# First projection tiles: products over two token tiles in turn, high parts split on ScalarE in halves, no zero products between the loads

## The chip, the cores and the metric

The kernel runs on one core of one Trainium2 chip, as a single launch. The time is device time in microseconds (us); lower is better. A core has five engines that run side by side, each with its own queue of instructions in order: TensorE (PE; its weight loads are listed as PEld), VectorE (DVE), ScalarE (ACT), GpSimd (POOL) and SyncE (SP), which here issues all transfers between the device memory and the on-chip memory.

## The reference

Two branches over the same 2048 tokens of 448 numbers, mixed by a gate per token. Only the first projection, `x @ wqkv`, and the gate's product are touched by the change.

```python
def _A_ref(x, wqkv, wo):                     # x: 1 x 2048 x 448, wqkv: 448 x 1344
    H, Dh, W, dil = 16, 28, 8, 2
    qkv = (x @ wqkv).reshape(B, S, 3, H, Dh) ...
    q, k, v = qkv[0], qkv[1], qkv[2]
    # each token attends to itself and the 7 tokens at distances 2, 4, ... 14 before it
    logits = einsum("bhsd,bhswd->bhsw", q, kg) * Dh ** -0.5    # masked before the start
    o = einsum("bhsw,bhswd->bhsd", softmax(logits), vg)
    return o.reshape(B, S, D) @ wo
def _B_ref(x, w1, b1, w2, b2):               # w1: 448 x 1792, w2: 1792 x 448
    h = x @ w1 + b1
    return relu(h) ** 2 @ w2 + b2
g = sigmoid((x * gate_w).sum(-1))
return g * A(x) + (1 - g) * B(x)
```

## The kernel before, in words

**Products in three parts.** TensorE gets its operands rounded to a shorter float format. To keep the accuracy, each operand is split into a high part (the rounded number) and a low part (the number less its high part), and each product is made as high x high, high x low and low x high, summed in one accumulator. Making the high part is a copy (ScalarE, or VectorE in one place); making the low part is a subtraction on VectorE. The 448 rows of a contraction are three tiles of 128 (k = 0, 1, 2) and a last one of 64 rows; the last one of two accumulators is computed side by side, each in one half of the array (`side_by_side`, line 189).

**Tokens.** The 2048 tokens are four chunks of 512 (`CH`), each four token tiles of 128. A product of the projection takes one token tile as the stationary operand (128 x 128) and 450 columns of the weights as the moving one (448 of q, then 2 columns with the gate's weights).

**The start, up to about 13 us: lines 621 to 657 and `qkv_first`.** SyncE loads, in this order: the q weights of k = 0 (`wqraw`), the tokens of k = 0 in two halves of 256 (`xraw`, line 637), the q weights and tokens of k = 1, then of k = 2, then the last 64 rows of both, then the weights of k and v. Meanwhile TensorE makes 13 products of a tile of zeros (`warm`, line 625). The weights are split as they land: the high part on ScalarE (line 648, `wqh`), the low part on VectorE (line 651, `wql`). The tokens' high part `x.h` is made on VectorE (line 650), but for the second half of k = 0 on ScalarE (line 654); their low part `x.l` on VectorE (lines 652 and 655). `qkv_first` (line 251) opens four accumulators, one for each token tile of the first chunk, and makes for k = 0, 1, 2 the three products of tile 0, then those of tile 1, tile 2 and tile 3 (line 258), 12 products for each k. After k = 0 and k = 1 come two products and one product on zeros (`FILL`, line 261). Then follow the last rows of q, all of k and v for these tiles (`run`, line 236, by `side_by_side`).

**The rest.** Chunks 1 to 3 of the projection follow; q, k and v go to device memory and come back regrouped for the attention, whose products run on GpSimd and whose sums on VectorE, from about 74 us on. TensorE goes on with the second branch (accumulators named h and b) and at the end with the output product (a). The order of the work outside TensorE is written out by a recording layer: `advance(dt)` moves a clock that counts the planned TensorE time, and `at` and `when` put ScalarE, VectorE and transfer work into the queues when that clock reaches a due time. The clock counts `12 * MM448` for each k of the first stage and nothing for products on zeros.

Of the kernel before, what the change touches and what calls it, by code (L numbers as in the profile page):

```python
# [9 lines left out]
AF = mybir.ActivationFunctionType  # L10
# [4 lines left out]
P = 128  # L15
# [7 lines left out]
CH = 512  # L23
NQ = D + 2
# [23 lines left out]
DEFER = 2  # L48
ORDER = (3, 0, 1, 2)
WARM = 13  # L50
FILL = (2, 1, 0)
PP_BUFS = 4
ST_BUFS = 3
BT_BUFS = 8
# [3 lines left out]
def gated_mix_kernel(ctx: ExitStack, tc: tile.TileContext, xT, wqkv, w1, w2, wo, b1, b2, out):  # L58
    nc = tc.nc

    def f32(ap):
        return ap.bitcast(F32)
# [37 lines left out]
    biasp = ctx.enter_context(tc.tile_pool(name="biasp", bufs=1))  # L100
    b1z = biasp.tile([P, 16], F32, name="b1z")
    b1t, none = b1z[:, :NF], b1z[0:1, 15:16]
    nc.vector.memset(none, 0.0)

    ctx.enter_context(tc.manual_schedule())
    nc.gpsimd.memset(mask, 0.0)
# [26 lines left out]
    def x_tiles(c, pool):  # L133
        return X([pool.tile([P, 2, CH], F32R, tag=f"x{j}", name=f"x{c}_{j}") for j in range(4)])
# [11 lines left out]
    def ps(tag, name):  # L146
        return psum.tile([P, 512], F32, tag=tag, name=name, bufs=4)
# [21 lines left out]
    def block(b):  # L169

        o = (0, NP, NP + D)[b]
        return slice(o, o + ncols(b))
# [45 lines left out]
    def full(x, acc, tl, b, ks=range(3)):  # L218
        sl, n = slice(tl * P, tl * P + P), block(b)
        r = []  # L220
        for k in ks:
            r += [(acc, x.h[k][:, sl], wqh[:, k, n]), (acc, x.h[k][:, sl], wql[:, k, n]),
                  (acc, x.l[k][:, sl], wqh[:, k, n])]
        return r

    def last(x, acc, tl, b):

        sl = slice(tl * P, tl * P + P)
        n = block(1) if b == 2 else slice(0, ncols(b))
        h, l = w7h[:, n], w7l[:, n]  # L230
        return [(acc, x.x7[:, sl], h), (acc, x.x7[:, sl], l), (acc, x.x8[:, sl], h)]

    def accs(c, b, tls, tags):
        return [Acc(t, f"qkv{c}_{tl}_{b}", ncols(b)) for t, tl in zip(tags, tls)]

    def run(c, todo, steps):


        a = 0
        for e, done, *turns in steps:  # L240
            side_by_side(todo[0][a:e], todo[1][a:e])
            while a < e:
                advance(min(12, e - a) * MM448)
                a = min(a + 12, e)
            for t in turns:
                t() if callable(t) else turn(*t)
            for b, tl, acc in done:
                assert acc.todo == 0
                qkv_evacuate(acc.pt, c, tl, b)

    def qkv_first(x):

        four = range(4)
        q = accs(0, 0, four, "bbbb")
        for k in range(3):
            for i in four:
                for j, (acc, a, w) in enumerate(full(x, q[i], i, 0, (k,))):
                    nc.tensor.matmul(acc.pt[:, :NQ], a, w, start=k == j == 0, stop=False)  # L258
            advance(12 * MM448)
            for _ in range(FILL[k]):  # L260
                nc.tensor.matmul(warm[:, :2 * P], zero[:, :P], zero, start=True, stop=True)
        for acc in q:
            acc.todo = 3
        k = accs(0, 1, four, "mmmm")
        t = [sum((last(x, a[i], i, b) for i in four), []) for b, a in ((0, q), (1, k))]
        f = [full(x, k[i], i, 1) for i in four]
        run(0, [t[0] + f[0] + f[1] + f[2] + f[3], t[1] + f[2] + f[3] + f[0] + f[1]],
            [(3, [(0, 0, q[0])], (k[0], k[0])),
             (12, [(0, i, q[i]) for i in (1, 2, 3)], (k[1], k[1])),
             (24, [], (k[0], k[2])), (33, [], (k[1], k[3])),  # L270
             (39, [(1, 0, k[0]), (1, 2, k[2])]), (48, [(1, 1, k[1]), (1, 3, k[3])])])
        v = accs(0, 2, four, "bbbb")
        f, l = [full(x, v[i], i, 2) for i in four], [last(x, v[i], i, 2) for i in four]
        run(0, [f[0] + l[0] + f[2] + l[2] + f[1] + f[3], f[1] + l[1] + f[3] + l[3] + f[0] + f[2]],
            [(15, [], (v[0], v[1])), (24, [], (v[2], v[3])),
             (33, [(2, 0, v[0]), (2, 1, v[1])]), (42, [(2, 2, v[2]), (2, 3, v[3])])])
# [195 lines left out]
    def advance(dt):  # L472
        clock["pe"] += dt
        while due := [x for x in later if x[0] <= clock["pe"]]:
            item = min(due, key=lambda x: x[0])
            later.remove(item)
            item[1]()
        if not clock["on"]:
            clock["att"] = clock["pe"]
            return  # L480
        while clock["att"] < clock["pe"]:
            try:
                r = next(att)
            except StopIteration:
                clock["on"] = False
                return
            if r is None:
                clock["att"] = clock["pe"]
                return
            clock["att"] += r  # L490


    def raw_tile(name):
        return rawp.tile([P, 4, 512], F32, tag="raw", name=name)
# [126 lines left out]
    warm = ps("m", "warm")  # L621
    zero = prodp.tile([P, 2 * P], F32R, tag="pp", name="zero", bufs=PP_BUFS)
    nc.vector.memset(f32(zero), 0.0)
    for _ in range(WARM):
        nc.tensor.matmul(warm[:, :2 * P], zero[:, :P], zero, start=True, stop=True)

# [2 lines left out]
    rx = raw_tile("xraw0")  # L629
# [16 lines left out]
    x = x_tiles(0, xap)  # L646
    for k in range(3):
        nc.scalar.activation(wqh[:, k, :NQ], raws[0][:, k, :NQ], AF.Copy)
        parts = (slice(0, 256), slice(256, CH)) if k == 0 else (slice(0, CH),)
        nc.vector.tensor_copy(x.h[k][:, parts[0]], rx[:, k, parts[0]])  # L650
        nc.vector.tensor_sub(wql[:, k, :NQ], raws[0][:, k, :NQ], f32(wqh[:, k, :NQ]))
        nc.vector.tensor_sub(x.l[k][:, parts[0]], rx[:, k, parts[0]], f32(x.h[k][:, parts[0]]))
        for cols in parts[1:]:
            nc.scalar.activation(x.h[k][:, cols], rx[:, k, cols], AF.Copy)
            nc.vector.tensor_sub(x.l[k][:, cols], rx[:, k, cols], f32(x.h[k][:, cols]))
    split_full(raws[0][:, 3, :NQ], w7h[:, :NQ], w7l[:, :NQ])
    split_x78(rx[:, 3], x.x7, x.x8)
# [79 lines left out]
    for c in range(4):  # L737
        x = xs[c]
        if c == 0:
            qkv_first(x)  # L740
        else:
            qkv_two(x, c, 0, copies=c == 3)
            qkv_two(x, c, 2, (mlp_one, mlp_two) if c == 3 else (), c == 3)
        if c == 1:
            st_["spilled"] = 0
            clock["on"] = True
            clock["att"] = clock["pe"] - 1.0
            advance(0.0)
        if c == 3:
            st_["spilled"] = 1  # L750
# [279 lines left out]
    c, x = ORDER[0], xm[3]  # L1030
# [8 lines left out]
    for g in range(2, 2 * NF):  # L1039
        i, f = g // (NF // 2), g % (NF // 2) * 2  # L1040
# [4 lines left out]
        if not f:  # L1045
            x, slots = X([nxt[j][0] for j in range(4)]), [nxt[j][1] for j in range(4)]
# [113 lines left out]
```

## Time and profile before

| | |
|---|---|
| time, median of 3 runs | 416.32 us (416.09, 416.32, 417.35) |
| time of the profiled execution | 416.65 us |
| span of the profiled execution, first to last record | 414.9 us (1.75 us of the time lie outside it) |
| TensorE busy | 409.9 us, 99% of the span |
| VectorE, ScalarE, GpSimd busy | 256.3, 210.8, 268.8 us |
| moved by transfers | 73.76 MB |

A row of the timeline gives the start in us, the time in us, the engine, the line of the program, the operation, output<-input, shapes and how many in a row are merged; behind it in brackets stands how long the engine had been idle and what ended that. TensorE's products are pipelined, so the start of the next one, not the listed duration, tells how long one holds the engine.

### The profile page before, as it was taken

What the parts mean: (1) busy time and instruction counts of PE and PEld (TensorE: products, weight loads), DVE (VectorE), ACT (ScalarE), POOL (GpSimd) and SP (SyncE); (2) the same over time, 40 slices, a digit from 0 to 9 for tenths busy, and PEclk for the clock granted to TensorE, in tenths of its full rate; (3) what the DMA queues carried; (4) which work ended last, traced back from release to release, by engine and by line L of the source; (5) the groups of instructions that cost most, each with busy time, mean ns of one, the idle gap of its engine ahead of it and who ended that gap; (6) DMA issues with size and microseconds to landing.
All of it is one profiled execution on the core that took longest, in us unless ns stands there. A gap on an engine that the chain in (4) does not pass through costs nothing.

```text
span 414.9 us, 9326 instructions
## 1 busy us (share of the span) xinstructions
PE 409.9 (99%) x3838; PEld 371.4 (90%) x3838; DVE 256.3 (62%) x404; ACT 210.8 (51%) x473; POOL 268.8 (65%) x167
## 2 busy tenths in 40 slices
PE   8999999999999999999999999999999999999996
PEld 7999999989998888888888888989898888888996
DVE  5520523276676767777656797879586677891354
ACT  3642656488766465444565534544652254346540
POOL 0000000874988999999989898999899986850000
PEclk9999999999999999999999999999999999999999
DMA  7999799989164307554112659764145612168304
GB/s 236 358 335 302 229 360 297 359 274 320 47 204 177 127 2 257 208 183 151 38 49 99 222 162 264 197 142 145 27 169 183 231 46 78 52 164 146 94 0 179
DMA packets 65611, 73.76 MB, mean 178 GB/s; under 512 B 32352, under 2 KB 58528, under 8 KB 65184
## 3 DMA queue, kind: packets, MB, share of 16 engines
q1 hardware_dynamic: 65568, 73.16, 54.1%
q8 instruction: 30, 0.49, 0.5%
q14 instruction: 13, 0.11, 0.1%
HBM read 45.71 MB, written 28.25 MB: 178 GB/s over the span
## 4 chain that ended last, share of the span: by engine, by line
PE 94%; DVE 3%; DMA 1%; ACT 1%; issue 0%; SPq 0%; DVEq 0%
PE b L189 32%; PE h L189 32%; PE qkv L189 21%; PE a L189 7%; PE qkv L258 1%; DMA xraw<-xT 1%; DVE lg L334 1%; PE a L934 1%; DVE bt L813 0%; DVE w1l L516 0%; DVE h L613 0%; PE last L934 0%; ACT copy L511 0%; ACT st L208 0%; SPq L637 0%
## 5 line engine op out<-in xcount | busy, mean ns | idle before, releaser
L333 POOL TENSOR_TENSOR qk<-q,k 128x896 f32<-128x896 f32 x64 | 135.1, 2150 | 85.0 <-DMA k<-k_d 80.2
L340 POOL TENSOR_TENSOR av<-lg,v 128x896 f32<-128x896 f32 x64 | 119.9, 1974 | 6.2 <-DVE lg L334 4.7
L189 PE MATMUL qkv<-wqh,x 64*128 64x448 f32 (+1 forms) x528 | 89.6, 361 | 0.1
L613 DVE TENSOR_TENSOR h<-h,h 128x512 fp32r<-128x512 f32 x56 | 38.4, 687 | 62.1 <-ACT h L616 61.8
L189 PEld LDWEIGHTS qkv<-wqh,x 64*128 64x128 f32 x528 | 70.1, 184 | 1.6 <-DVE qkv L199 0.5
L189 PE MATMUL qkv<-wql,x 64*128 64x448 f32 (+1 forms) x264 | 69.6, 360 | 0.0
L334 DVE TENSOR_REDUCE lg<-qk 128x32 f32<-128x896 f32 x64 | 67.2, 1075 | 2.7 <-POOL qk L333 2.7
L348 DVE TENSOR_REDUCE o<-av 128x112 f32<-128x896 f32 x64 | 66.5, 1070 | 1.5 <-POOL av L340 1.2
L189 PE MATMUL b<-w2ah,h 64*128 64x448 f32 x448 | 66.5, 360 | 0.4 <-DVE h L613 0.4
L189 PE MATMUL b<-w2bh,h 64*128 64x448 f32 x448 | 66.2, 360 | 0.0
L614 ACT ACTIVATE h<-h,b1z 128x512 f32<-128x512 f32 x56 | 36.7, 656 | 44.1 <-PE h L189 44.1
L189 PEld LDWEIGHTS b<-w2ah,h 64*128 64x128 f32 x448 | 41.8, 184 | 4.6 <-DVE h L613 0.9
L189 PEld LDWEIGHTS b<-w2bh,h 64*128 64x128 f32 x448 | 42.0, 184 | 3.8 <-ACT h L565 0.3
L189 PEld LDWEIGHTS qkv<-wql,x 64*128 64x128 f32 x264 | 41.5, 184 | 0.5
L208 ACT ACTIVATE st<-qkv 128x448 f32<-128x448 f32 x48 | 24.6, 543 | 32.7 <-PE qkv L189 27.6
L189 PE MATMUL b<-w2bl,h 64*128 64x448 f32 x224 | 40.7, 358 | 0.0
L189 PE MATMUL b<-w2al,h 64*128 64x448 f32 x224 | 40.5, 358 | 0.0
L615 ACT ACTIVATE h<-h 128x512 fp32r<-128x512 f32 x56 | 33.6, 599 | 1.7
L616 ACT ACTIVATE h<-h 128x512 f32<-128x512 f32 x56 | 33.2, 594 | 0.0
L565 ACT ACTIVATE h<-h 128x4 fp32r<-128x4 f32 (+1 forms) x35 | 7.2, 206 | 43.3 <-PE b L189 43.1
L189 PE MATMUL h<-x,w1h 64*128 64x512 f32 x168 | 28.5, 386 | 0.0
L189 PE MATMUL h<-x2b,w1h 64*128 64x512 f32 x168 | 28.3, 388 | 0.0
(148 smaller groups left out, 706.9 us busy)
## 6 DMA issues: line engine op xcount, KB each, us to landing
k<-k_d SPq DMA_DIRECT2D x8, 840.0 KB, 6.6
v<-v_d SPq DMA_DIRECT2D x8, 840.0 KB, 4.8
x_d<-x SPq DMA_DIRECT2D x11, 512.0 KB, 5.1
q_d<-st SPq DMA_DIRECT2D x8, 448.0 KB, 4.1
k_d<-st SPq DMA_DIRECT2D x8, 448.0 KB, 3.8
v_d<-st SPq DMA_DIRECT2D x8, 448.0 KB, 7.2
w1raw<-w SPq DMA_DIRECT2D x4, 896.0 KB, 10.0
q<-q_d SPq DMA_DIRECT2D x8, 448.0 KB, 3.5
```

The costliest lines, as they stand in the source:

```text
L189: nc.tensor.matmul(acc.pt[:, :acc.n], a[rows], w[rows], start=acc.todo == acc.all, stop=acc.todo == 1)
L208: nc.scalar.activation(st[:, :, t % 2], pt[:, :D].rearrange("p (g c) -> p g c", g=G), AF.Copy)
L258: nc.tensor.matmul(acc.pt[:, :NQ], a, w, start=k == j == 0, stop=False)
L333: nc.gpsimd.tensor_mul(pr, q[:, s:s + 1].to_broadcast([P, W, C]), k[:, s:s + W])
L334: pending.append(lambda: nc.vector.tensor_reduce(lg[:, s], pr.rearrange("p w (h d) -> p w h d", h=HG), axis=AX.X, op=ALU.add))
L340: nc.gpsimd.tensor_mul(pr.rearrange("p (h d) w -> p w h d", h=HG), lg[:, s][:, :, :, None].to_broadcast([P, W, HG, DH]), v[:, s:s + W].rea ...
L348: nc.vector.tensor_reduce(o[:, g * C:(g + 1) * C], pr, axis=AX.X, op=ALU.add)
L565: nc.scalar.activation(ap, f32(ap), AF.Copy)
L613: nc.vector.tensor_sub(hl, pt, f32(hh))
L614: ops += [lambda pt=pt, r=r: nc.scalar.activation(pt, pt, AF.Relu, bias=b1t[:, f + r:f + r + 1]), lambda pt=pt, hh=hh: nc.scalar.activatio ...
L615: lambda pt=pt, hh=hh: nc.scalar.activation(hh, pt, AF.Square),
L616: lambda pt=pt, r=r, low=low: (nc.scalar.activation(pt, pt, AF.Square), at(delays[r], low))]
```

## The change

1. In `qkv_first`, for each k, the products are made for the token tiles 0 and 1 in turn (high x high of tile 0, high x high of tile 1, high x low of 0, of 1, low x high of 0, of 1) and then for tiles 2 and 3 in the same way.
2. The products on zeros after k = 0 and k = 1 are gone. The 13 products at the start stay.
3. For k = 1 and 2 the tokens' high part is made on ScalarE, in two halves of 256 tokens, and the low part on VectorE in the same halves. For k = 0 the first half stays on VectorE. The loads are not changed: the tokens of k = 1 and 2 land as one transfer each.
4. The memset of one zero (`none`) stands behind that of the zero tile on VectorE, in place of ahead of it.

ScalarE's queue at the start becomes: q weights k = 0, tokens k = 0 second half, weights k = 1, tokens k = 1 first and second half, weights k = 2, tokens k = 2 first and second half, and on as before. VectorE's loses the two token copies of k = 1 and 2, and has four subtractions of 256 tokens in place of two of 512. The order on GpSimd and SyncE, and that on all engines behind this stage, is the same.

```diff
-FILL = (2, 1, 0)
...
-    nc.vector.memset(none, 0.0)
...
-            for i in four:
-                for j, (acc, a, w) in enumerate(full(x, q[i], i, 0, (k,))):
-                    nc.tensor.matmul(acc.pt[:, :NQ], a, w, start=k == j == 0, stop=False)
+            for two in ((0, 1), (2, 3)):
+                for j, prods in enumerate(zip(*(full(x, q[i], i, 0, (k,)) for i in two))):
+                    for acc, a, w in prods:
+                        nc.tensor.matmul(acc.pt[:, :NQ], a, w, start=k == j == 0, stop=False)
             advance(12 * MM448)
-            for _ in range(FILL[k]):
-                nc.tensor.matmul(warm[:, :2 * P], zero[:, :P], zero, start=True, stop=True)
...
     nc.vector.memset(f32(zero), 0.0)
+    nc.vector.memset(none, 0.0)
...
     for k in range(3):
         nc.scalar.activation(wqh[:, k, :NQ], raws[0][:, k, :NQ], AF.Copy)
-        parts = (slice(0, 256), slice(256, CH)) if k == 0 else (slice(0, CH),)
-        nc.vector.tensor_copy(x.h[k][:, parts[0]], rx[:, k, parts[0]])
+        halves = (slice(0, 256), slice(256, CH))
+        for i, cols in enumerate(halves):
+            if k == i == 0:
+                nc.vector.tensor_copy(x.h[k][:, cols], rx[:, k, cols])
+            else:
+                nc.scalar.activation(x.h[k][:, cols], rx[:, k, cols], AF.Copy)
         nc.vector.tensor_sub(wql[:, k, :NQ], raws[0][:, k, :NQ], f32(wqh[:, k, :NQ]))
-        nc.vector.tensor_sub(x.l[k][:, parts[0]], rx[:, k, parts[0]], f32(x.h[k][:, parts[0]]))
-        for cols in parts[1:]:
-            nc.scalar.activation(x.h[k][:, cols], rx[:, k, cols], AF.Copy)
+        for cols in halves:
             nc.vector.tensor_sub(x.l[k][:, cols], rx[:, k, cols], f32(x.h[k][:, cols]))
```

## The prediction

> **What bounds the kernel now.** I began with the page: busy times first, then the chain that ended last.
>
> ```profile
> PE 409.9 (99%) x3838; PEld 371.4 (90%) x3838; DVE 256.3 (62%) x404; ACT 210.8 (51%) x473; POOL 268.8 (65%) x167
> PE 94%; DVE 3%; DMA 1%; ACT 1%; issue 0%; SPq 0%; DVEq 0%
> ```
>
> TensorE is busy for all but 5 us of the span and carries 94% of the chain. So whatever TensorE loses at the start comes back at the end, unless something later waits for another engine anyway. The view of windows shows where that could be:
>
> ```profile
> 40.00:50.00 10.00, 10.00 (x103) 10.00 (x101) 4.82 (x13) 7.48 (x19) 0.00 (x0) 1.00 0.72 237
> 84.00:92.00 8.00, 7.86 (x76) 6.83 (x76) 6.59 (x16) 6.00 (x15) 6.99 (x4) 1.00 0.79 239
> 92.00:240.00 148.00, 148.00 (x1398) 132.12 (x1396) 104.10 (x143) 85.80 (x191) 134.04 (x79) 1.00 0.43 150
> 240.00:252.00 12.00, 11.63 (x112) 9.96 (x110) 11.14 (x17) 4.24 (x10) 11.75 (x8) 1.00 0.62 167
> 252.00:405.00 153.00, 153.00 (x1460) 136.11 (x1458) 102.84 (x143) 73.23 (x165) 105.41 (x61) 1.00 0.45 129
> ```
>
> The second figure is TensorE's busy time. It is idle for 0.14 us at 84 to 92 and for 0.37 us at 240 to 252, and not at all in the long stretches. I take what it waits for there to be work that earlier products release, so that it shifts with them; the rival on a gain given back prices the other case. The change lies wholly before 13.4 us, and the chain in order of time shows what sets that stretch:
>
> ```profile
> 2.60 4.31 DMA xraw<-xT
> 6.94 0.04 DVE x L650
> 6.97 0.31 issue
> 7.28 0.62 DVE wql L651
> 7.90 0.61 DVE x L652
> 8.52 0.04 issue
> 8.56 2.28 PE qkv L258 x10
> 10.84 0.12 PE warm L261
> 10.96 2.46 PE qkv L258 x12
> 13.42 69.34 PE qkv L189 x674
> ```
>
> The tokens of k = 1 land at 6.91; VectorE then copies them, splits the weights and subtracts, one behind the other, and TensorE has them at 8.56. From there it runs without a stop for 69 us. So the stage costs what three VectorE steps behind one landing cost, then 22 products and one on zeros. TensorE's own rows:
>
> ```profile
> 4.16 0.64 PE L258 MATMUL qkv<-wqh,x 128*128 128x450 f32 x1
> 4.65 0.74 PE L258 MATMUL qkv<-wql,x 128*128 128x450 f32 x1
> 5.19 0.95 PE L258 MATMUL qkv<-wqh,x 128*128 128x450 f32 x2
> 5.94 0.48 PE L258 MATMUL qkv<-wql,x 128*128 128x450 f32 x1
> 6.26 0.56 PE L258 MATMUL qkv<-wqh,x 128*128 128x450 f32 x2
> 7.67 0.41 PE L261 MATMUL warm<-zero 128*128 128x256 f32 x2
> 7.92 0.37 PE L258 MATMUL qkv<-wqh,x 128*128 128x450 f32 x1
> 8.12 0.37 PE L258 MATMUL qkv<-wql,x 128*128 128x450 f32 x1
> 8.56 0.68 PE L258 MATMUL qkv<-wqh,x 128*128 128x450 f32 x2
> 10.68 0.28 PE L261 MATMUL warm<-zero 128*128 128x256 f32 x1
> 10.80 0.36 PE L258 MATMUL qkv<-wqh,x 128*128 128x450 f32 x1
> 13.35 0.47 PE L189 MATMUL qkv<-w7h,x 64*128 64x450 f32 x2
> ```
>
> Read the starts. From 5.19 two products take 0.75, so 0.375 each; from 6.26 on the seven left of k = 0 take 1.41, so 0.20 each; the change of pace falls at about 6.2. Until then TensorE is slow, whatever it is given. Lost are 0.28 at k = 0 (4.16 to 5.19 is 1.03 for two products in place of 0.75), 0.25 and 0.12 for the products on zeros, and 0.35 at k = 1 (7.92 to 10.68 is 2.76 for twelve products in place of 2.41). What feeds them:
>
> ```profile
> 3.36 0.58 ACT L648 ACTIVATE wqh<-wqraw 128x450 fp32r<-128x450 f32 x1 [1.33 <-DMA wqraw<-wqkv]
> 3.65 0.29 DVE L650 CAST x<-xraw 128x256 fp32r<-128x256 f32 x1 [2.48 <-DMA xraw<-xT]
> 3.97 0.63 DVE L651 TENSOR_TENSOR wql<-wqraw,wqh 128x450 fp32r<-128x450 f32 x1
> 4.51 0.42 DVE L652 TENSOR_TENSOR x<-xraw,x 128x256 fp32r<-128x256 f32 x1
> 5.36 0.42 ACT L654 ACTIVATE x<-xraw 128x256 fp32r<-128x256 f32 x1 [1.43 <-DMA xraw<-xT]
> 6.03 0.58 ACT L648 ACTIVATE wqh<-wqraw 128x450 fp32r<-128x450 f32 x1 [0.25 <-DMA wqraw<-wqkv]
> 7.48 0.58 ACT L648 ACTIVATE wqh<-wqraw 128x450 fp32r<-128x450 f32 x1 [0.87 <-DMA wqraw<-wqkv]
> 8.66 0.43 DVE L650 CAST x<-xraw 128x512 fp32r<-128x512 f32 x1 [0.16 <-DMA xraw<-xT]
> 9.48 0.58 ACT L115 ACTIVATE w7h<-wqraw 128x450 fp32r<-128x450 f32 x1 [1.42 <-DMA wqraw<-wqkv]
> 10.32 0.63 ACT L115 ACTIVATE x<-xraw 128x512 fp32r<-128x512 f32 x1 [0.26 <-DMA xraw<-xT]
> 11.59 1.80 DVE L116 TENSOR_TENSOR wql<-wqraw,wqh 128x448 fp32r<-128x448 f32 x3
> ```
>
> **k = 0: two tiles in turn.** The second product becomes high x high of tile 1, which needs only the first half of the tokens (3.65 + 0.29 = 3.94) and the weights' high part (3.36 + 0.58 = 3.94). Six slow products start at 4.16, 4.53, 4.91, 5.28, 5.66 and 6.03. The weights' low part is ready at 3.97 + 0.63 = 4.60, before the third; the tokens' at 4.51 + 0.42 = 4.93, before the fifth. Tile 2 needs the second half, ready at 5.36 + 0.42 = 5.78. The pace changes inside the sixth product, so the seventh starts at 6.31 and the twelfth ends at 7.51, against 7.67: 0.16 gained. That is the 0.28 of waiting, halved because slow time is given back as fast time.
>
> **k = 1: ScalarE in halves.** ScalarE is free at 6.03 + 0.58 = 6.61 and starts on the landed tokens at about 6.94. The half of 256 costs 0.42 by the row at 5.36, so the first is ready at 7.36 and, with the 0.05 that the wake-up at 8.56 shows (7.90 + 0.61 = 8.51), usable at 7.41: just ahead of 7.51. The second half is ready at 7.78 and wanted by the seventh product at 8.7. On VectorE the weights' low part no longer stands behind a token copy: it starts when ScalarE's high part is there, at 6.64, and ends at 7.27. The tokens' low halves take 0.42 each (row at 4.51): 7.41 to 7.83 and to 8.25; wanted by the fifth product at 8.31 and the eleventh at 9.5. So nothing waits: twelve products from 7.51 to 9.92, against 10.68. 0.76 gained so far, of which 0.25 are the two products on zeros and 0.35 the wait for the low part.
>
> **k = 2.** The one product on zeros is gone: 9.92 against 10.80, 0.88. The new ScalarE queue puts this k's weights behind the second token half: 7.78 in place of 7.48, done at 8.36; their low part at about 9.02. The tokens land at 8.66 and are high at 9.08 and 9.50, low at 9.54 and 9.96. All of it is wanted between 9.92 and 11.9, so the 0.30 lie under cover of at least 0.8. If they didn't, they would cost at most 0.30. Twelve products and the step to the half rows took 10.80 to 13.35 = 2.55, so L189 starts at 12.47.
>
> **What comes next.** The last rows' weights at ScalarE start at 9.50 in place of 9.48; their tokens land at 10.32 as before. VectorE then subtracts the k weights until 11.59 + 1.80 = 13.39; the first of them is wanted after 24 half-row products (12 pairs of 0.20), at 14.9. Nothing new is late. The moved memset of one number frees the zero tile up to 0.1 earlier; I take 0, with 0 to 0.1 as bounds, because the first real product wants the tokens at 3.94 anyway.
>
> **The sum.** 0.88 off the path: 416.65 - 0.88 = 415.77 on the profiled execution, which lay 0.33 above the median of the runs; on the median 416.32 - 0.88 = 415.4. The one cost that no row shows is the pace of full-array products that go to two accumulators in turn. A zero product of 256 columns takes 0.12 (10.68 to 10.80) and one of 450 takes 0.201, so 0.42 ns a column and 14 ns fixed. If turns hide the 14 ns, about 24 fast products gain another 0.33; if they double them, as much is lost. I take none, because the rows of pairs cost the same 0.20 for a pair as a single one here. The gain is then 0.55 to 1.3. About 0.3% (1.25 us) is what a measurement of this kernel can tell from no change.
>
> **The clock's rule.** The windows list the granted clock as 1.00 throughout, and only the spacing, 0.375 before 6.2 and 0.20 after it, shows the slow start here. The Trainium skill, TensorE: Matmul & The Clock Gate, section "Part 1: The HAM clock gate", says that the array runs at half rate until about 3.4 us of sustained work in a window that runs freely, so that the switch falls differently from run to run. The spacing agrees with a half rate; one trace can't show the free window. Whatever moves the switch, a late one at 9.6 gives: before, twelve slow products and the wait from 4.16 to 8.94, two slow zeros to 9.4, L189 at about 14.5; after, twelve slow ones to 8.66, two and a half more to 9.6, L189 at about 14.0. So 0.5 gained in place of 0.88, 415.8.
>
> **Rivals.** *Slower: TensorE falls back to the slow pace*, since the products on zeros no longer bridge the loads. It decides if TensorE is idle for clearly longer than the 0.4 us before 8.56, which it bore without falling back. Price: up to 24 products at 0.175 more each, 4.2: 416.32 - 0.88 + 4.2 = 419.6. Against it: the new gap at 7.51 is 0.1 at most, unless the tokens of k = 1 land much later. 0.08.
> *Gain given back later*: TensorE comes earlier to the stretch at 84 to 92, where transfers or VectorE might not follow. Against it: at 40 to 50 the transfers are busy for 0.72 only, so they wait for work and would shift with it; 416.3. Together with the late switch, 0.17.
> *More than the sum*: turns hide the fixed part, or the first product starts earlier: gain 1.2 to 1.3, 415.1. Nothing in the rows speaks for it beyond the 14 ns. 0.25.
>
> **How the numbers follow.** The forecast, 415.4, has 0.50. The three runs lie 1.26 apart, so two medians differ by some 0.5 without a cause; about a third of the forecast's chance thereby reads as over 1.25 gained, and most of the third rival's. Faster 0.38, slower 0.08, same 0.54. The range, 414.5 to 416.8, holds the bounds of the gain (415.8 to 415.0) with that scatter, and the gain given back; it leaves out the fall-back and the tails.
>
> **What would show it.** Right: L189 at about 12.5 in place of 13.35; no wait above 0.1 between 4.16 and there; ScalarE's k = 1 halves at about 6.9 and 7.4; first product of k = 1 at 7.5; everything later shifted alike. Wrong: products 0.375 apart after 7 us; a TensorE wait for ScalarE ahead of k = 1 or 2; new idle time at 84 to 92 or 240 to 252.

## The result, and the profile after

The changed kernel takes 415.70 us (median of 15 runs, 415.30 to 416.14), the kernel before 416.46 us (15 runs, 416.09 to 417.35): 0.76 us less, a ratio of 0.9981 with a 95% interval of 0.9974 to 0.9988. The gain is clear of zero, though it is below the 0.3% under which the prediction saw no measurable change; 415.4, a gain of 0.88, was forecast.

The profiled execution of the changed kernel took 415.92 us, its span is 414.1. The chain in order of time begins and ends so:

```profile
...
0.87 0.27 DVE zero L621
1.14 0.04 DVE b1z L622
1.18 0.02 issue
1.20 3.14 PE warm L624 x13
4.34 8.64 PE qkv L258 x36
12.98 69.34 PE qkv L187 x674
...
411.13 0.45 DVE bt L815
```

Before, the chain reached back through VectorE to the landing of the tokens of k = 1. Now TensorE is on it from its first zero product on: all 36 products of the stage follow each other, with no engine and no transfer between them. The 69.34 us behind it are the same to the hundredth, and start 0.44 earlier (12.98 for 13.42). TensorE's rows:

```profile
4.14 0.99 PE L258 MATMUL qkv<-wqh,x 128*128 128x450 f32 x2
4.93 0.95 PE L258 MATMUL qkv<-wql,x 128*128 128x450 f32 x2
5.67 1.69 PE L258 MATMUL qkv<-wqh,x 128*128 128x450 f32 x4
7.17 0.60 PE L258 MATMUL qkv<-wql,x 128*128 128x450 f32 x2
7.61 0.97 PE L258 MATMUL qkv<-wqh,x 128*128 128x450 f32 x4
8.42 0.56 PE L258 MATMUL qkv<-wql,x 128*128 128x450 f32 x2
...
12.42 0.56 PE L258 MATMUL qkv<-wqh,x 128*128 128x450 f32 x2
12.91 0.47 PE L187 MATMUL qkv<-w7h,x 64*128 64x450 f32 x2
```

No row carries a wait. But from 5.67 four products take 1.50: TensorE is at the slow pace of 0.375 until about 7.2, 1 us longer than in the profile of before. For k = 1 and 2 the feeding engines stand close to the forecast:

```profile
6.19 0.58 ACT L647 ACTIVATE wqh<-wqraw 128x450 fp32r<-128x450 f32 x1 [0.22 <-DMA wqraw<-wqkv]
6.95 0.73 ACT L654 ACTIVATE x<-xraw 128x256 fp32r<-128x256 f32 x2 [0.18 <-DMA xraw<-xT]
7.58 0.56 ACT L647 ACTIVATE wqh<-wqraw 128x450 fp32r<-128x450 f32 x1
8.80 0.73 ACT L654 ACTIVATE x<-xraw 128x256 fp32r<-128x256 f32 x2 [0.65 <-DMA xraw<-xT]
6.81 0.63 DVE L655 TENSOR_TENSOR wql<-wqraw,wqh 128x450 fp32r<-128x450 f32 x1 [0.37 <-ACT wqh L647]
7.40 0.76 DVE L657 TENSOR_TENSOR x<-xraw,x 128x256 fp32r<-128x256 f32 x2
```

ScalarE starts on the landed tokens at 6.95 and has both halves at 7.68; the low halves are there at 8.16, while the products that want them start at 8.8 and later. Further on, TensorE's busy time in the two places with idle time, looked at 0.8 earlier, is as it was (before: 7.86 of 8 and 11.63 of 12):

```profile
83.20:91.20 8.00, 7.87 (x76) 6.88 (x74) 6.23 (x15) 6.28 (x15) 5.73 (x3) 1.00 0.75 224
239.20:251.20 12.00, 11.65 (x110) 9.94 (x106) 11.14 (x17) 4.24 (x10) 11.74 (x8) 1.00 0.63 171
```

The last VectorE step starts 0.65 earlier (411.13 for 411.78), while the stage gives 0.44. The other 0.21 come at 322 to 347, where the kernel before ran its pieces a little slower in that execution; why is open. The first fence is the chain of before, the second that of after; 24 of these h products take 2.72 elsewhere, 24 b products 2.40.

```profile
322.35 2.83 PE h L189 x24
...
332.07 2.77 PE h L189 x24
334.84 2.48 PE b L189 x24
```

```profile
334.24 2.52 PE b L187 x24
```

From the first half-row product to the last VectorE step, all 13 profiled executions of this study take 398.15 to 398.64 us, with before (398.43) and after (398.22) inside; so what the stage gains goes through to the end. The spread of 0.49 among equal or nearly equal programs I take for scatter; it is as large as what the single parts of the change are worth, so these are read from the rows of the stage.

### The profile page after: what moved, and what is told of

Read it like the earlier page. It is cut to its first block, busy times and chain, and to the rows that moved or that the text cites. A ratio compares the mean times of both kernels' runs of the same rounds, so it can differ in the third digit from the quotient of the medians.

```text
span 414.1 us, 9324 instructions
## 1 busy us (share of the span) xinstructions
PE 409.4 (99%) x3835; PEld 374.4 (90%) x3835; DVE 255.8 (62%) x404; ACT 211.8 (51%) x477; POOL 268.8 (65%) x167
## 4 chain that ended last, share of the span: by engine, by line
PE 96%; DVE 2%; ACT 1%; issue 0%; DVEq 0%
PE b L187 32%; PE h L187 32%; PE qkv L187 21%; PE a L187 7%; PE qkv L258 2%; DVE lg L332 1%; PE warm L624 1%; PE a L936 1%; DVE bt L815 0%; DVE w1l L514 0%; DVE h L611 0%; PE last L936 0%; ACT copy L509 0%; ACT st L206 0%; DVE w17l L514 0%
## 5 line engine op out<-in xcount | busy, mean ns | idle before, releaser
L187 PE MATMUL h<-x1b,w1h 64*128 64x512 f32 x168 | 28.2, 386 | 0.0
```

The source lines that it names most:

```text
L187: nc.tensor.matmul(acc.pt[:, :acc.n], a[rows], w[rows], start=acc.todo == acc.all, stop=acc.todo == 1)
```

## The experiments

Each time is compared with runs of the kernel before made beside it on the same chip. One profile per kernel shows one execution only, so the verdicts go by all the runs of a kernel. The ratio is not the quotient of the two medians, and in places the two differ (in experiment 5, 0.9976 and 0.9984). Experiments 4 and 5 keep the memset of one number where it was before; the eleventh has that move alone.

**1. Zero products gone, alone.** `- for _ in range(FILL[k]): matmul(warm, zero ...)`

> Before, with only the products on zeros between the loads left out. Theory (the stage is a chain: what is gained ahead of a wait is lost in the wait): the second tile of zero products goes, but the third product of k = 1 still waits for VectorE's low part at 8.56, so only the one product after k = 1 is gained: the half-row products start 0.12 earlier than before (13.35 to 13.23), time -0.1 us. Rival (each part brings its own share, 0.25 + 0.12): 0.37 earlier, 12.98. Fall-back rival: products 0.375 us apart after 8 us and several us more.

416.56 against 416.65 us, ratio 0.9999 (0.9990 to 1.0008). The median is where the chain theory had it; the rival's 0.37 us (ratio 0.9991) lies just inside the interval, so the times alone don't decide. Its TensorE rows show the place:

```profile
7.23 0.36 PE L258 MATMUL qkv<-wqh,x 128*128 128x450 f32 x1
8.19 0.44 PE L258 MATMUL qkv<-wqh,x 128*128 128x450 f32 x1 [0.60 <-DVE x L648]
8.63 0.47 PE L258 MATMUL qkv<-wql,x 128*128 128x450 f32 x1
9.23 0.69 PE L258 MATMUL qkv<-wqh,x 128*128 128x450 f32 x2
9.76 0.36 PE L258 MATMUL qkv<-wql,x 128*128 128x450 f32 x1
9.96 0.56 PE L258 MATMUL qkv<-wqh,x 128*128 128x450 f32 x2
```

Freed of the zeros, TensorE stands idle where they were: it waits for VectorE's copy, then for its low part (8.63 to 9.23). In this execution the tokens of k = 1 reached VectorE 0.67 later (7.61) than in the profile of before, so the half-row products came at 13.85, not at the 13.23 expected. The pace is 0.20 again behind the gap (9.76 to 9.96).

**2. Turns alone.** `- for i in four: / + for two in ((0, 1), (2, 3)):` with zeros and VectorE's whole copies kept.

> Before, with only the order of products changed to two token tiles in turn; zero products and VectorE's whole token copies stay. Theory (chain): k = 0 ends at 7.51, zeros to 7.76, and the low part that comes at 8.56 is now wanted by the fifth product, at 8.56, so its wait goes too: half-row products at about 12.84, time -0.5 us. Rival (each part brings its own share): only the 0.16 of k = 0, 13.19, time -0.16 us. Both for a pace that changes at 6.2 as in the profile of before; where it changes 1 us later, some 0.4 later.

416.33 against 416.65, ratio 0.9993 (0.9984 to 1.0001): -0.32 us, between the two forecasts, and not told apart. The half-row products stood at 12.97, in an execution whose first tokens landed 0.64 late and whose pace changed before 5.3: two products take 0.42 from there on.

```profile
5.32 0.58 PE L259 MATMUL qkv<-wql,x 128*128 128x450 f32 x2
5.74 0.97 PE L259 MATMUL qkv<-wqh,x 128*128 128x450 f32 x4
```

**3. Halves alone.** `+ for cols in halves: nc.scalar.activation(x.h[k][:, cols], ...)`

> Before, with only the token splits of k = 1 and 2 on ScalarE in halves; order tile by tile and zero products stay. Theory (chain): k = 0 and its zeros end at 7.92 as before, the low half is there at 7.88 for the third product, nothing waits: half-row products at 13.0, time -0.35 us. Rival (VectorE's copy was hidden behind the slow products anyway): no gain.

416.03 against 416.65, ratio 0.9988 (0.9980 to 0.9997). The stage fell as worked out:

```profile
7.91 0.37 PE L258 MATMUL qkv<-wqh,x 128*128 128x450 f32 x1
8.12 0.37 PE L258 MATMUL qkv<-wql,x 128*128 128x450 f32 x1
8.33 0.56 PE L258 MATMUL qkv<-wqh,x 128*128 128x450 f32 x2
...
13.01 0.47 PE L189 MATMUL qkv<-w7h,x 64*128 64x450 f32 x2
```

The third product of k = 1 follows the second by 0.21, where before it came 0.44 later. This is the one part whose gain alone is clear of zero. The median moved 0.62, more than the 0.35 of the stage; the interval holds both.

**4. Changed kernel without halves** (turns, no zeros, VectorE's whole copies).

> The changed kernel without its halves: two tiles in turn, no zero products, tokens split whole on VectorE for k = 1 and 2. Theory (chain): k = 0 ends at 7.51, the third product waits to 7.95 and the fifth from 8.35 to 8.56, so half-row products at about 12.72, time -0.6 us, 0.25 behind the changed kernel. Rival (halves add nothing beside the turns): as the changed kernel, -0.75 us. Where the pace changes 1 us later, TensorE comes after the low part and the two theories agree.

416.05 against 416.65, ratio 0.9984 (0.9975 to 0.9993): -0.60. The medians can't tell the two forecasts apart. The half-row products stood at 13.12, not at 12.72. In the rows two waits have to be kept apart:

```profile
6.87 0.56 PE L259 MATMUL qkv<-wqh,x 128*128 128x450 f32 x2
7.86 0.66 PE L259 MATMUL qkv<-wqh,x 128*128 128x450 f32 x2 [0.43 <-DVE x L649]
8.35 0.63 PE L259 MATMUL qkv<-wql,x 128*128 128x450 f32 x2
8.91 1.09 PE L259 MATMUL qkv<-wqh,x 128*128 128x450 f32 x4
```

The 0.43 in brackets is not the theory's: in this execution the tokens of k = 1 reached VectorE at 7.29, 0.35 later than in the profile of before, and some 0.33 of that wait would be there with halves too (an estimate: a half of 0.42 and the 0.05 of the wake-up behind 7.29 give 7.76 for 7.86). The wait ahead of the fifth product is the theory's: two products from 8.35 to 8.91 take 0.56 in place of 0.40, since the tokens' low part is done only at 8.86 (8.17 and 0.69). The third product's wait, to 7.95, did not appear by itself. So VectorE's whole copies still cost TensorE time here, against the rival, but most of the gain is there without the halves.

**5. Changed kernel without turns** (halves, no zeros, tile by tile).

> The changed kernel without its turns: products tile by tile, no zero products, tokens split in halves on ScalarE. Theory (chain): k = 0 ends at 7.67 with the 0.28 of waiting still in it, then nothing waits: half-row products at 12.63 for a pace that changes at 6.2, time -0.7 us, 0.16 behind the changed kernel. Rival (the turns carry the gain): no better than -0.4 us.

415.81 against 416.49, ratio 0.9976 (0.9961 to 0.9991): -0.68. By the medians the turns are not needed for the gain; the 0.16 of k = 0 is lost in the scatter. In the profile the half-row products came at 13.21, not at 12.63:

```profile
6.38 0.91 PE L258 MATMUL qkv<-wqh,x 128*128 128x450 f32 x2
7.12 0.38 PE L258 MATMUL qkv<-wql,x 128*128 128x450 f32 x1
...
13.21 0.48 PE L189 MATMUL qkv<-w7h,x 64*128 64x450 f32 x2
```

Two products from 6.38 take 0.74, so the pace changed at about 7.1, nearly as late as in the profile of after, whose 12.91 is the number to set beside. Of the 0.30 between them k = 0 makes 0.13 (its end at 8.15 for 8.02). The other 0.17 are 24 products that stand 0.207 apart in place of 0.200; the ninth run has the same 0.207 with turns, so the order is not the cause, and the cause stays open.

**6. One zero product at the start.** `- WARM = 13 / + WARM = 1`

> The changed kernel with 1 product on zeros at the start in place of 13. Theory (the pace changes some 5 to 6 us after TensorE begins to be busy): it stays slow until about 9, half-row products at 13.5 to 14.5, time +0.8 to +1.6 us against the changed kernel. Rival (it changes at a fixed time after the launch, or at a time of its own): as the changed kernel.

416.85 against 416.49, ratio 1.0008 (0.9999 to 1.0017). Set against the changed kernel's 0.9981 above, that is 0.27%, 1.1 us slower: the theory's size. The eighth run, in the same comparison, has the changed kernel with other data at the start, and there the distance between the medians is 1.16 us. The profiled execution (416.36 us, half-row products at 12.94 and not at 13.5 to 14.5) doesn't show it:

```profile
4.07 1.09 PE L258 MATMUL qkv<-wqh,x 128*128 128x450 f32 x2 [2.29 <-DVE x L652]
4.95 0.95 PE L258 MATMUL qkv<-wql,x 128*128 128x450 f32 x2
5.70 1.67 PE L258 MATMUL qkv<-wqh,x 128*128 128x450 f32 x4
7.20 0.59 PE L258 MATMUL qkv<-wql,x 128*128 128x450 f32 x2
7.63 0.98 PE L258 MATMUL qkv<-wqh,x 128*128 128x450 f32 x4
```

Here the pace changes at 7.2, 3.1 us after the first product of the stage; in the profile of after also at 7.2, but there TensorE had been busy for 6.0 us, since its first zero product. So the change of pace does not come after a fixed length of work, and the theory's form was wrong for this execution. Nor does it come at a fixed time after the start, as one rival had it: it fell before 5.3 in the second run and at about 6.0 in the eighth. That most executions of this kernel change later, as the median asks, is argued and not shown.

**7. Tokens of k = 1 loaded late.** Loads in the order `w1, w2, x2, x1`.

> The changed kernel with the tokens of k = 1 loaded behind the weights and tokens of k = 2, so that TensorE has a gap of 1 us or more between k = 0 and k = 1 and no products on zeros in it. Theory (a gap of 1 us does not bring the slow pace back): tokens land at about 8.6, products 0.20 apart from 9.1 on, half-row products at about 14.1, time +1.2 to +1.6 us against the changed kernel. Fall-back rival of the prediction: products 0.375 apart after the gap, half-row products at 16 to 18, time +3.5 us or more.

417.37 against 416.49, ratio 1.0019 (1.0010 to 1.0028): 0.38%, 1.6 us, above the changed kernel.

```profile
7.00 0.56 PE L258 MATMUL qkv<-wqh,x 128*128 128x450 f32 x2
9.04 0.67 PE L258 MATMUL qkv<-wqh,x 128*128 128x450 f32 x2 [1.47 <-ACT x L661]
...
9.96 0.96 PE L258 MATMUL qkv<-wqh,x 128*128 128x450 f32 x4
10.76 0.56 PE L258 MATMUL qkv<-wql,x 128*128 128x450 f32 x2
...
14.05 0.47 PE L187 MATMUL qkv<-w7h,x 64*128 64x450 f32 x2
```

After 1.47 us without work, and no zeros in it, four products take 0.80 (9.96 to 10.76). A gap of 1.47 us did not bring the slow pace back in this execution, and the median lies by the theory's 1.2 to 1.6 us, not by the rival's 3.5. So the fall-back rival is refuted for gaps up to about 1.5 us; the profile of after has no gap in the stage.

**8. Ones in place of zeros at the start.** `- memset(f32(zero), 0.0) / + 1.0`

> The changed kernel with ones in place of zeros in the tile of the 13 products at the start. Theory (the pace depends on TensorE being busy, not on what it multiplies): no difference beyond 0.2 us. Rival (products on zeros count less towards the change of pace): the pace changes at about 4.6, k = 1 waits for its tokens only, half-row products at 12.4, time -0.4 us against the changed kernel.

415.69 against 416.49, ratio 0.9982 (0.9973 to 0.9991): as the changed kernel. What the start products multiply makes no difference that is seen. In its profile the pace changed at about 6.0 (four products from 5.73 to 6.63) and the half-row products stood at 12.55.

**9. The changed kernel again, 10. with the zeros back, 11. the moved memset alone.**

> The changed kernel once more, beside the next two on the same chip. Theory (TensorE-bound from k = 1 on, gain set by when the pace changes): time -0.5 to -0.9 us against before, half-row products between 12.4 and 13.0, the later the later the pace changes. Rival (part of the -0.76 us seen was scatter of the runs): -0.3 us or less.

> The changed kernel with the three products on zeros put back. Theory (with turns and halves nothing waits, so each product on zeros costs what it takes): 0.37 us slower than the changed kernel, half-row products 0.37 later for the same change of pace. Rival (they fall into a wait for the tokens of k = 1): 0.12 slower or less.

> Before, with only the memset of one number moved behind that of the zero tile. Theory: no difference, 0 +- 0.15 us, the zero products start 0.1 earlier at most; so it also shows how far two equal kernels lie apart in this measurement. Rival (earlier zero products bring the change of pace forward): -0.2 us or more.

Against 416.68 us: 416.12 (ratio 0.9987, 0.9976 to 0.9997), 416.36 (0.9990, 0.9978 to 1.0003) and 416.70 (0.9992, 0.9967 to 1.0017). The gain comes back at 0.56 us. The zeros cost 0.24 by the medians, between both forecasts and not told apart; in the profile of the tenth run they take 0.25 (7.98 to 8.23) and 0.13 (10.63 to 10.76), with no wait beside them that they could fall into, which speaks for the theory. The memset alone moves the median by 0.02, but its interval is wide, -1.4 to +0.7 us, so it doesn't exclude the rival's 0.2. In its profile the half-row products came at 13.87, 0.52 later than in that of before: VectorE started on the tokens of k = 1 at 7.43 in place of 6.94, and TensorE waited behind it. In the profile of the ninth the pace changed at about 7.4 and the half-row products came at 13.42, past the 13.0 expected: its first product had started at 4.56, 0.42 late, for want of tokens, so that k = 0 ended 0.34 later than in the profile of after (8.36 for 8.02), and its next 24 products stood 0.207 apart, another 0.17.

```profile
4.56 1.09 PE L258 MATMUL qkv<-wqh,x 128*128 128x450 f32 x2 [0.22 <-DVE x L652]
5.44 0.95 PE L258 MATMUL qkv<-wql,x 128*128 128x450 f32 x2
6.19 1.51 PE L258 MATMUL qkv<-wqh,x 128*128 128x450 f32 x4
7.54 0.56 PE L258 MATMUL qkv<-wql,x 128*128 128x450 f32 x2
```

No version beat the changed kernel clear of the scatter; without the turns, and with ones in place of zeros, the times are as good.

## Why the prediction was right, point by point

- **The stage carries the whole change, and its gain goes through to the end**: shown. What follows the stage takes 398.15 to 398.64 us in every profile, whenever it begins (12.55 to 14.05).
- **k = 0**: the working held, one number did not. The twelfth product was to end at 7.51 and ended at 8.02 (7.61 and two products on). The change of pace, taken at 6.2 from the one profile of before, fell at 7.2 here. That is the step which makes 12.47 into 12.91; from 8.02 on the 24 products and the step to the half rows took 4.89 for 4.96 forecast. In the eighth run, the same program but for the data of the start products, the pace changed at 6.0 and the half-row products came at 12.55, beside the 12.47. With the late change two of the signs named for being right were missed in the profile of after (half-row products at 12.91, not about 12.5; first product of k = 1 at 8.02, not 7.5), and the slow pace ran past the 7 us named as a sign of being wrong. It was no fall-back: the products stand 0.375 apart from the start of the stage, with no fast stretch before.
- **k = 1**: right. ScalarE's half started at 6.95 (forecast 6.94), and nothing waited. The two halves took 0.73, not 0.84, as they overlap by 0.1. That the VectorE chain behind the landing holds TensorE up is shown by the third run (halves alone, the wait gone) and the fourth (without halves, 0.16 of it still there). But halves and turns work on the same wait: the halves make the low part earlier, the turns want it two products later. By the medians most of the gain is there without the halves (0.60) or without the turns (0.68).
- **k = 2**: right. The weights' split began at 7.58 for 7.78, and what it began later than before (0.1) stayed under cover. It needs tokens that land in time: in the eighth run ScalarE started on them at 9.47, not 8.80, and TensorE's weight load waited 0.2 for them.
- **The zeros**: their 0.25 and 0.12 count only once nothing else waits. Alone they bring 0.09 us, not told from nothing. The three parts alone, 0.09, 0.32 and 0.62, sum to more than the 0.76 of all, as parts of the same wait would; given the intervals, that sum is a hint and no proof.
- **Turns between accumulators**: the pace of 0.20 is the same, so the 14 ns are neither hidden nor doubled, and the first product started at 4.14 for 4.16; the rival "more than the sum" falls.
- **The late change of pace** was priced at a gain of 0.5 for a change at 9.6 in both kernels. The 0.44 between the two profiles is not that case, near as it lies: it sets a kernel before that changed at 6.2 against a changed kernel that changed at 7.2. By the rows of before, a change at 7.2 would have put its half-row products at about 13.46 (an estimate), a gain of 0.55. So what is gained depends on the draw. The tokens' landing is drawn too: VectorE started on those of k = 1 at 6.94 in the profile of before, at 7.43 in the eleventh run and at 7.61 in the first, behind the same loads. The sum of 0.88 took both from one execution. That the medians came near it, with 0.76 and then 0.56, is in part luck; how both are spread over the runs that have no profile is not known. The Trainium skill, TensorE: Matmul & The Clock Gate, section "Part 1: The HAM clock gate", has the rate rise after a busy window that runs freely and fall after an idle one of about 3.4 us. The changes from less than 4.1 us (second run) to 6.2 us (ninth run) after the first product, and the 1.47 us gap without a fall, agree; in the sixth run, idle for 2.29 us until 4.07, the change came 3.1 us later, a little under that window of about 3.4. No run here had an idle time long enough to show the fall.
- **Gain given back later**: refuted by the two windows and by what follows the stage, which takes as long as before.

## What to carry to other kernels

Where TensorE is the bound from some point on, time before that point is worth its full length, and the chain of waits tells which engine owns it: here three VectorE steps behind one landing. Such a wait can go in two ways, by having the operand earlier (two halves on an idle engine) or by wanting it later (two tiles in turn), and the second way on top of the first added nothing that the medians show. Leaving out filler work ahead of the wait gained nothing measurable while the wait stood (0.09 us); take the wait away first. One profile is one draw: the pace at the start and the landings vary by as much as the gain that is argued about, or more, so put a range on each and let medians of many runs decide.

## What the runs showed of the hardware that was not expected

The change from 0.375 to 0.20 us for a product of 450 columns fell between less than 5.3 and 7.4 us after the start in these executions of nearly equal programs. Behind it the products stand 0.200 apart in some stretches and 0.207 in others, even within the profile of before (six products from 9.07 to 10.27 take 1.20, six from 11.61 to 12.85 take 1.24); over 24 products that is 0.17 us, and its cause is open. The first tokens reached VectorE between 3.59 and 4.31 us, for the same loads in the same order. Two ScalarE copies of 256 columns in a row take 0.73 us, not twice 0.42.
